# Steady groups: two visits of scores with seven PSUM banks each, one bank shared by both heads of a pair, in place of visits with six and eight

## The chip, the cores and the metric

The kernel runs on one core of a Trainium2 chip. Its time is the device time of one execution in microseconds (us), as a median over several runs. Before the change it is 344.38 us, the median of four runs from 344.21 to 344.92.

## What is computed

Sliding-window attention with ALiBi bias for 8 batches of 8 heads, 576 positions of 64 features each, and behind it a gated feed-forward block over the 4608 resulting rows of 512 features. Cut to what matters:

```python
scores = scale * q @ k.T                      # scale 1/8
mask = (rel >= 0) & (rel < 128)               # rel = query - key
attn = exp(scores + bias) under the mask, divided by its sum over the keys
x = attn @ v                                  # (4608, 512) over all heads
out = (gelu(x @ w_gate) * (x @ w_val)) @ w_out
```

## The kernel before

Engines: PE multiplies matrices into PSUM, ACT takes exponentials, gelu and copies, DVE does elementwise work, SP issues output transfers and transposing transfers. PSUM is one pool of eight banks of 128 x 512 fp32. Every result of PE takes a bank from it, `bank()`, and gives it back when its last reader is done; a new result waits for the reader whose bank it is given. The order on every engine is the order in which the code is written.

The feed-forward block runs over nine groups `g` of 512 rows. A group has twelve pairs of gate and value tiles (`gate_val`, L514: eight matmuls of 512 columns and two banks each; gelu on ACT, L520; the product with the value tile on DVE, L521) and four output tiles (`out_part`, L550: twelve matmuls of 512 columns into one bank; the copy out of PSUM by DVE or ACT, L555). The store of a finished output tile (L540, on SP) is issued at the start of the next call of `out_part`.

Attention for later batches is put between these output tiles, so that PE has work while ACT and DVE do theirs. A steady group (g = 2 to 5, batch b = g + 2) ends with the list that `steps(g)` gives: one output tile; the products of the batch before with its values (`values`, L392); a first visit of `scores` for pair 0; an output tile; a visit for pairs 1 to 3; an output tile; a visit for all four pairs; the sums of probabilities (`add`, on DVE); an output tile. The number 4 stands for one output tile (four calls' worth of three matmuls). In the next group, after three pairs of gate and value tiles, `sums4` (L334) takes the column sums.

Keys are taken in blocks of 128, n = 0 to 4, each with the 192 queries of its window (64 for the last block). `scores(b, s, cs)` covers blocks 0 and 1 for s = 0 and blocks 2, 3 and 4 for s = 1, for the pairs of heads in `cs`. For each pair it takes two banks, one for each head. Matmuls (L187, 64 keys by up to 192 queries) come in fours: head i of the pair takes the half i of PE's rows, and half x of the key block takes half x of PE's columns and of the bank's partitions. Then ACT takes the exponential of each bank (L192, 384 columns for s = 0, 448 for s = 1) into the probabilities `P`, and DVE multiplies both heads of the pair by the mask `emask` (L195). In banks, the three visits of a steady group take two, six and eight.

A PE matmul can be made to wait for another PE matmul through `relay`: a no-operation on another queue (SP in steady groups) waits for the first matmul, and the second one waits for it (`depends`). Before the change, only the products use this (L320), where one bank is written by both halves of PE's rows, one after the other.

Of the kernel before, what the change touches and what calls it, by code (L numbers as in the profile page):

```python
# [27 lines left out]
def kernel(  # L28
# [10 lines left out]
    nc = tc.nc  # L39
# [23 lines left out]
    def bank():  # L63
        return psum.tile([128, 512], FP32, name="ps")


    def keep_busy(ps, n, w=64):
        for _ in range(n):
# [17 lines left out]
    emask = consts.tile([128, H, 448], BF16, name="emask")  # L86
# [4 lines left out]
    qT, kT = ([consts.tile([128, 4, 640], BF16, name=f"{nm}T{i}") for i in range(2)]  # L91
              for nm in "qk")
# [81 lines left out]
    def prob(b):  # L174
        return Ps[b % 2].rearrange("p (c i) n -> p c i n", i=2)


    def keys(b, c, m):
        if b < 2:
            return kT[b][:, c, 64 * m:64 * m + 64]  # L180
        at = 512 * (m // 2) + 128 * c + 64 * (m % 2)
        return kT[b % 2].rearrange("p c x -> p (c x)")[:, at:at + 64]


    def score(b, c, i, m, q0, n, out, first=True):
        half = slice(64 * i, 64 * i + 64)
        nc.tensor.matmul(  # L187
            out=out, lhsT=keys(b, c, m)[half, :], rhs=qT[b % 2][half, c, q0:q0 + n],
            start=first, stop=True, skip_group_check=not first)

    def exp(dst, src):
        nc.scalar.activation(out=dst, in_=src, func=AF.Exp, scale=0.125)  # L192

    def mask(dst, m):
        nc.vector.tensor_tensor(out=dst, in0=dst, in1=m, op=ALU.mult)  # L195


    def scores(b, s, cs, later=None):
        pss = []
        for c in cs:  # L200
            ps = [bank(), bank()]
            pss.append(ps)
            for n in ((0, 1), (2, 3, 4))[s]:
                w, col = 64 if n == 4 else 192, 192 * (n - 2 * s)
                for x in (0, 1):
                    for i in (0, 1):
                        score(b, c, i, 2 * n + x, 128 * n + 64 * x, w,
                              ps[i][64 * x:64 * x + 64, col:col + w])
        w = (384, 448)[s]
        for c, ps in zip(cs, pss):  # L210
            dst = prob(b)[:, c, :, 64 + 384 * s:64 + 384 * s + w]
            for i in (0, 1):
                exp(dst[:, i, :], ps[i][:, 0:w])
            args = (dst, emask[:, 2 * c:2 * c + 2, 0:w])
            if later is None:
                mask(*args)
            else:
                later.append(args)

# [12 lines left out]
    def scores0(cs, pss, between=None):  # L234
        for c, ps in zip(cs, pss):
            for n in range(3):
                for x in (0, 1):
                    q0 = 128 * n + 64 * x
                    w = min(192, 384 - q0)
                    for i in (0, 1):  # L240
                        score(0, c, i, 2 * n + x, q0, w,
                              ps[i][64 * x:64 * x + 64, 192 * n:192 * n + w], False)
        for c, ps in zip(cs, pss):
            for i in (0, 1):
                exp(prob(0)[:, c, i, 0:512], ps[i])
                if i == 0 and between:
                    between()


    def scores0_rest(cs, later):  # L250
        pss = []
        for c in cs:
            ps = [bank(), bank()]
            pss.append(ps)
            for n, skip, w, col in ((4, 0, 64, 0), (2, 64, 128, 64), (3, 0, 192, 192)):
                for x in (0, 1):
                    for i in (0, 1):
                        score(0, c, i, 2 * n + x, 128 * n + 64 * x + skip, w,
                              ps[i][64 * x:64 * x + 64, col:col + w])
        for c, ps in zip(cs, pss):  # L260
            dst = prob(0)[:, c, :, 512:896]
            for i in (0, 1):
                exp(dst[:, i, :], ps[i][:, 0:384])
            later.append((dst.rearrange("p i (n x) -> p i n x", x=192),
                          emask[:, 2 * c:2 * c + 2, 0:192].unsqueeze(2).to_broadcast((128, 2, 2, 192))))
# [42 lines left out]
    def in_turn(mms):  # L308
        by_group = [[m for m in mms if m[0] == g] for g in range(4)]
        return [ms[n] for n in range(max(map(len, by_group))) for ms in by_group if n < len(ms)]  # L310

    def depends(use, on):
        tc.add_manual_dep(use.ins, on.ins.name, mybir.DependencyInfo(
            mybir.DependencyClass.Sync, mybir.DependencyReason.DATA), reason="one bank, two halves")

    def relay(mm, engine=nc.sync):
        by = engine.nop()  # L320
        depends(by, mm)
        return by

    def sums4(b, s):
        first, w = shape(b, s)
# [33 lines left out]
    def products(b, banks):  # L359
# [19 lines left out]
        for n, (_, x, u, c, m, q0, q1, col, to, lo, hi) in enumerate(todo):  # L379
            begun.setdefault(u, x)  # L380
            half = slice(64 * x, 64 * x + 64)
            for i in (0, 1):
                rows = slice(64 * i, 64 * i + 64)
                if isinstance(c, int):
                    h = 2 * c + i
                    out = pss[u][rows, to + q0 - lo:to + q1 - lo]
                    lhsT = vb[b % 2][half, m // 2, 64 * h:64 * h + 64]
                else:
                    out = pss[u][rows, to:to + (c.stop - c.start) * (hi - lo)].rearrange(
                        "p (c x) -> p c x", x=hi - lo)[:, :, q0 - lo:q1 - lo]  # L390
                    lhsT = ones64[half, :]
                mm = nc.tensor.matmul(  # L392
                    out=out, lhsT=lhsT, rhs=prob(b)[half, c, i, col:col + q1 - q0],
                    start=all(t[2] != u for t in todo[:n]), stop=True, skip_group_check=True)
                if begun[u] != x and u in by:
                    depends(mm, by.pop(u))
            if begun[u] == x and all(t[1:3] != (x, u) for t in todo[n + 1:]):
                by[u] = relay(mm, nc.vector if b in (1, 2) else nc.sync)
# [82 lines left out]
    def products_rest():  # L481
        w = S - lo0
        pss = products(0, [(n, slice(2 * n, 2 * n + 2), lo0, S, 0) for n in (0, 1)] + [
            (2 + c // 2, c, lo0, S, w * (c % 2)) for c in range(4)])
        for n in (0, 1):
            nc.scalar.copy(out=recip[0][:, 2 * n:2 * n + 2, lo0:S],
                           in_=pss[2 + n][:, 0:2 * w].rearrange("p (c x) -> p c x", c=2))
        return pss
# [49 lines left out]
    def store():  # L538
        for args in stores:
            nc.sync.dma_start(**args)  # L540
        stores.clear()
# [63 lines left out]
    for h in (0, 2, 4, 6):  # L605
        for w, src in ((0, q), (1, k)):
            (nc.scalar if w and h == 0 else nc.sync).dma_start(  # L607
                out=raw[w][h // 4].rearrange("p (h x) -> p h x", h=4)[:, h % 4:h % 4 + 2, :],
# [24 lines left out]
    for x in (0, 1):  # L633
        half, to = slice(64 * x, 64 * x + 64), slice(64 * x, 64 * x + 192)
# [130 lines left out]
    pss = products_rest()  # L765
# [10 lines left out]
    for n in range(2):  # L776
        nc.gpsimd.dma_start(
            out=wo[:, 6 * n:6 * n + 6, :],
# [5 lines left out]
    for t in (qs[0], ks[0]):  # L784
# [5 lines left out]
    todo = {  # L790
        0: [("table",), ("s", 1, 0, (0, 1)), ("o", 0, 0, 0), ("o", 0, 1, 0), ("s", 1, 0, (2, 3)), ("o", 0, 0, 1), ("s", 1, 1, (0, 1)), ("o", 0, 1, 1), ("s", 1, 1, (2, 3), masks), ("pv+", 1, 0), 4, ("pv+", 1, 1), ("transposes", 2), 4],
        1: [("table",), ("s", 2, 0, (0, 1)), 3, ("s", 2, 0, (2, 3)), 2, ("s", 2, 1, (0, 1)), 2, ("s", 2, 1, (2, 3), masks), ("pv+", 2, 0), 3, ("pv+", 2, 1), 1, ("s", 3, 0, (0, 1)), 2, ("s", 3, 0, (2, 3)), 3, ("add", 3, 0), ("s", 3, 1, range(4))],
    }

    def steps(g):
        b = g + 2
        if g in todo:
            return todo[g]
        if b > B:
            return [16] if g < NG - 1 else [12, ("last", g)]  # L800
        if b == B:
            return [4, ("pv", b - 1), 12]
        return [("table",), 4, ("pv", b - 1), ("s", b, 0, (0,)), 4, ("s", b, 0, (1, 2, 3)), 4,
                ("s", b, 1, range(4)), ("add", b, 0), ("add", b, 1), 4]


    def exp_table():
        nc.scalar.preload_act_table_set("natural_log_exp_and_others")

    RUN = {"s": scores, "add": add, "sum4": sums4, "gather": gather, "spread": spread_dma, "pv": values, "pv+": values_and_sums,  # L810
           "masks": flush, "table": exp_table, "transposes": transposes_dma, "last": out_last, "o": out_half}

    for g in range(NG):
# [33 lines left out]
        for item in steps(g):  # L847
            if isinstance(item, int):
                out_part(g, item)
            else:  # L850
                RUN[item[0]](*item[1:])
        store()
# [35 lines left out]
```

## Time and profile before

| what | us |
|---|---|
| median of four runs | 344.38 |
| the profiled execution, its time | 344.47 |
| its span, first to last instruction | 342.7 |
| PE busy | 334.9 |
| DVE busy | 190.1 |
| ACT busy | 174.3 |
| POOL busy | 108.5 |
| matmuls of scores, L187 (656), busy | 19.0 |
| exponentials, L192 (128), busy | 55.9 |
| masks, L195 (60), busy | 34.8 |

The span is what the profile's instructions cover; the time adds what lies around it. Busy time counts instructions of an engine without their overlap; matmuls are pipelined and the profile models their ends. PE's clock was granted in full throughout (1.000).

The last part of the third steady group (g = 4), as the timeline has it:

| start, us | what |
|---|---|
| 195.58 | products of the batch before, and the visit of pair 0 |
| 197.57 | second output tile |
| 200.27 | visit of pairs 1 to 3, 24 matmuls, six banks |
| 200.89 | third output tile |
| 203.58 | visit of all pairs, 48 matmuls, eight banks |
| 204.77 | fourth output tile |
| 207.36 | gate and value tiles of the next group |

### The profile page before, as it was taken

How to read it: one execution, taken by the hardware profiler on the slowest of the kernel's cores; microseconds unless marked ns; L12 is line 12 of the kernel's file. 1: busy time of each engine (PE TensorE's matmuls, PEld its weight loads, DVE VectorE, ACT ScalarE, POOL GpSimd, SP SyncE). 2: the span in 40 equal slices, each digit the busy share in tenths (PEclk: the TensorE clock that was granted, in tenths of full speed). 3: DMA queues.
4: the chain of work that ended last, by engine and by line, in shares of the span. 5: the costliest groups of instructions: out<-in, count | busy, mean ns of one | idle time of the engine just before them, and what ended most of it. 6: DMA issues, size and time to landing. Idle time of an engine off the chain costs nothing.

```text
span 342.7 us, 8079 instructions
## 1 busy us (share of the span) xinstructions
PE 334.9 (98%) x3310; PEld 170.7 (50%) x3310; DVE 190.1 (55%) x331; ACT 174.3 (51%) x339; POOL 108.5 (32%) x147
## 2 busy tenths in 40 slices
PE   8889999999999999999999999999999999999996
PEld 6567655444544455445544554445444544444443
DVE  8779565535599555944595369636773313303420
ACT  6884597537894339333753366344823133224322
POOL 9874763581193193009500770050000000000000
PEclk9999999999999999999999999999999999999999
DMA  8999999999599999989987999587114110020002
GB/s 210 169 197 190 205 163 137 149 191 174 124 161 128 190 168 195 175 178 86 182 175 157 94 178 185 138 100 97 63 36 104 63 65 0 0 94 31 0 31 94
DMA packets 149737, 43.48 MB, mean 127 GB/s; under 512 B 133540, under 2 KB 142660, under 8 KB 149700
## 3 DMA queue, kind: packets, MB, share of 16 engines
q0 software_dynamic: 107424, 18.10, 68.5%
q1 hardware_dynamic: 39104, 18.69, 22.9%
q10 hardware_dynamic: 3172, 6.19, 8.1%
q8 instruction: 26, 0.43, 0.5%
q14 instruction: 11, 0.09, 0.1%
HBM read 43.65 MB, written 9.53 MB: 155 GB/s over the span
## 4 chain that ended last, share of the span: by engine, by line
PE 90%; ACT 6%; DMA 2%; SPq 1%; issue 0%; DVE 0%; ACTq 0%
PE ps L514 54%; PE ps L550 25%; PE ps L392 4%; ACT P L192 3%; PE ps L187 2%; DMA ks<-in_k_dram 2%; PE ps L570 2%; PE ps L334 1%; ACT osb L555 1%; SPq L607 1%; PE ps L584 1%; PE ps L143 1%; ACT rb L468 0%; ACT rb L467 0%; ACT L520 0%
## 5 line engine op out<-in xcount | busy, mean ns | idle before, releaser
L521 DVE TENSOR_TENSOR hT<-ps,gelu 128x512 bf16<-128x512 f32 (+3 forms) x119 | 74.1, 636 | 92.1 <-PE ps L514 80.7
L520 ACT ACTIVATE gelu<-ps 128x512 bf16<-128x512 f32 (+3 forms) x119 | 65.4, 558 | 103.5 <-PE ps L514 90.4
L514 PE MATMUL ps<-xT,wg 128*128 128x512 bf16 (+3 forms) x476 | 113.5, 359 | 0.6 <-DVE xT L471 0.3
L514 PE MATMUL ps<-xT,wv 128*128 128x512 bf16 (+3 forms) x476 | 113.4, 359 | 0.0
L550 PE MATMUL ps<-wo,hT 128*128 128x512 bf16 x396 | 90.4, 379 | 0.2
L514 PEld LDWEIGHTS <-wv 128*128 128x128 bf16 x476 | 45.3, 98 | 48.5
L514 PEld LDWEIGHTS <-wg 128*128 128x128 bf16 x476 | 44.7, 98 | 48.6 <-issue 0.6
L192 ACT ACTIVATE P<-ps 128x384 bf16<-128x384 f32 (+2 forms) x128 | 55.9, 549 | 15.2 <-PE ps L187 15.0
L550 PEld LDWEIGHTS <-hT 128*128 128x128 bf16 x396 | 37.2, 98 | 44.2
L195 DVE TENSOR_TENSOR P<-P,emask 128x768 bf16<-128x768 bf16 (+1 forms) x60 | 34.8, 588 | 22.9 <-ACT P L192 22.0
L101 POOL DMA_DIRECT2D vb<-in_v_dram x40 | 33.9, 874 | 7.4 <-DMA ks<-in_k_dram 3.9
L555 ACT COPY osb<-ps 128x512 f32<-128x512 f32 x28 | 16.8, 599 | 36.6 <-PE ps L550 36.5
L101 POOL DMA_DIRECT2D qs<-in_q_dram x30 | 25.2, 855 | 6.2 <-DMA wo<-in_moe_w_out_dram 4.4
L839 POOL COPY mark<-hT 1x2 bf16<-1x2 bf16 x4 | 0.7, 176 | 79.2 <-DVE hT L521 79.2
L101 POOL DMA_DIRECT2D ks<-in_k_dram x30 | 25.6, 891 | 0.0
L187 PE MATMUL ps<-qT,kT 64*64 64x192 bf16 (+2 forms) x656 | 19.0, 236 | 0.2
L392 PE MATMUL ps<-P,vb 64*64 64x64 bf16 (+2 forms) x752 | 17.8, 221 | 0.3 <-SPq L320 0.2
L449 DVE TENSOR_TENSOR xT<-ps,rb 128x512 bf16<-128x512 f32 (+3 forms) x29 | 14.3, 563 | 6.6 <-PE ps L392 6.6
L187 PEld LDWEIGHTS <-kT 64*64 64x64 bf16 x656 | 13.1, 106 | 9.8 <-issue 7.8
L392 PEld LDWEIGHTS <-vb 64*64 64x64 bf16 x752 | 14.9, 107 | 4.2 <-issue 2.7
L276 DVE TENSOR_TENSOR T<-P 64x1024 bf16<-64x1024 bf16 (+1 forms) x20 | 15.0, 751 | 0.4
L425 DVE TENSOR_TENSOR xT<-ps,rb 128x512 bf16<-128x512 f32 (+1 forms) x10 | 6.4, 638 | 6.8 <-ACT rb L420 6.7
(86 smaller groups left out, 170.8 us busy)
## 6 DMA issues: line engine op xcount, KB each, us to landing
out_dram<-osb SPq DMA_DIRECT2D x35, 256.0 KB
rb<-rd ACTq DMA_DIRECT2D x10, 576.0 KB
vb<-in_v_dram POOLq DMA_DIRECT2D x32, 128.0 KB, 6.8
qs<-in_q_dram POOLq DMA_DIRECT2D x24, 128.0 KB, 5.0
ks<-in_k_dram POOLq DMA_DIRECT2D x24, 128.0 KB, 6.9
wo<-in_moe_w_out_dram POOLq DMA_DIRECT2D x2, 768.0 KB, 14.7
wg<-in_moe_w_gate_dram POOLq DMA_DIRECT2D x5, 256.0 KB, 8.5
wv<-in_moe_w_val_dram POOLq DMA_DIRECT2D x5, 256.0 KB, 9.4
```

The costliest lines, as they stand in the source:

```text
L101: nc.gpsimd.dma_start(out=t[0:n, j, :].rearrange("p (h d) -> p h d", h=H), in_=src[b][:, 128 * j:128 * j + n, :].rearrange("h p d -> p h d"))
L187: nc.tensor.matmul(out=out, lhsT=keys(b, c, m)[half, :], rhs=qT[b % 2][half, c, q0:q0 + n], start=first, stop=True, skip_group_check=not f ...
L192: nc.scalar.activation(out=dst, in_=src, func=AF.Exp, scale=0.125)
L195: nc.vector.tensor_tensor(out=dst, in0=dst, in1=m, op=ALU.mult)
L276: nc.vector.tensor_tensor(out=to[half, :, 2 * n0 + x:2 * n1 + x - 1:2], in0=P[half, :, 3 * n0:3 * n1 - 2:3], in1=P[half, :, 3 * n0 + 1:3 * ...
L392: mm = nc.tensor.matmul(out=out, lhsT=lhsT, rhs=prob(b)[half, c, i, col:col + q1 - q0], start=all(t[2] != u for t in todo[:n]), stop=True, ...
L449: nc.vector.tensor_tensor(out=xT[:, c, at:at + e - a], in0=src, in1=recip[b][:, c, a:e], op=ALU.mult)
L514: nc.tensor.matmul(out=ps, lhsT=w[:, c, 128 * f:128 * (f + 1)], rhs=xT[:, c, t0 + lo:t0 + hi], start=begins, stop=(c == 3), skip_group_che ...
L520: nc.scalar.activation(out=gl[:, 0:n], in_=pg, func=AF.Gelu)
L521: nc.vector.tensor_tensor(out=hid[g][:, f, lo:hi], in0=pv, in1=gl[:, 0:n], op=ALU.mult)
L550: nc.tensor.matmul(out=acc[g], lhsT=hid[g][:, f, 128 * t:128 * (t + 1)], rhs=wo[:, f, :], start=(f == 0), stop=(f == NF - 1))
L555: (nc.vector.tensor_copy if g < B - 2 and t in by_dve.get(g, (0,)) else nc.scalar.copy)(out=osb, in_=acc[g])
```

## The change

The last two visits of a steady group are made by a new function, `scores7`. Each takes seven banks: six for pairs 1 to 3, and one, `both`, in which both heads of pair 0 stand side by side. Visit s = 0 computes blocks 0 and 1 of pairs 1 to 3, as before, and block 2 of pair 0; visit s = 1 computes blocks 2 to 4 of pairs 1 to 3 and blocks 3 and 4 of pair 0. Head 0 writes its part of `both` first, then its share of pairs 1 to 3; head 1 takes the same pieces with pair 0 at the end. A relay on SP holds head 1's first matmul into `both` until head 0's last one is done. ACT takes the exponential of `both` last, as one instruction over both heads (2 x 192 columns, then 2 x 256). Pair 0's second mask covers 448 columns of each head and is made in visit s = 1, after the others.

The first visit of the group and all other groups are as before. `depends` and `relay` are moved up in the file without a change.

```diff
+    def scores7(b, s):
+        both, pss = bank(), [[bank(), bank()] for _ in range(3)]
+        todo = ([], [])
+        for i in (0, 1):
+            ns, w = (((2, 192),), 192) if s == 0 else (((3, 192), (4, 64)), 256)
+            for n, m in ns:
+                todo[i].append((0, n, m, both, w * i + 192 * (n - ns[0][0])))
+            mine = [(c, n, 64 if n == 4 else 192, pss[c - 1][i], 192 * (n - 2 * s))
+                    for c in (1, 2, 3) for n in ((0, 1), (2, 3, 4))[s]]
+            todo[i][:] = mine + todo[i] if i else todo[i] + mine
+        last = None
+        for n in range(len(todo[0])):
+            for x in (0, 1):
+                for i in (0, 1):
+                    c, m, w, ps, col = todo[i][n]
+                    half = slice(64 * i, 64 * i + 64)
+                    mm = nc.tensor.matmul(
+                        out=ps[64 * x:64 * x + 64, col:col + w], lhsT=keys(b, c, 2 * m + x)[half, :],
+                        rhs=qT[b % 2][half, c, 128 * m + 64 * x:128 * m + 64 * x + w],
+                        start=True, stop=True)
+                    if ps is both and i == 0:
+                        last = mm
+                    if ps is both and i and last is not None:
+                        depends(mm, by)
+                        last = None
+            if last is not None and todo[0][n][3] is both and (
+                    n + 1 == len(todo[0]) or todo[0][n + 1][3] is not both):
+                by = relay(last)
+        w = (384, 448)[s]
+        for c, ps in zip((1, 2, 3), pss):
+            dst = prob(b)[:, c, :, 64 + 384 * s:64 + 384 * s + w]
+            for i in (0, 1):
+                exp(dst[:, i, :], ps[i][:, 0:w])
+            mask(dst, emask[:, 2 * c:2 * c + 2, 0:w])
+        n, at = ((192, 448), (256, 640))[s]
+        exp(prob(b)[:, 0, :, at:at + n], both[:, 0:2 * n].rearrange("p (i x) -> p i x", i=2))
+        if s:
+            dst = prob(b)[:, 0, :, 448:896]
+            mask(dst, emask[:, 0:2, 0:448])
+
+
...
-        return [("table",), 4, ("pv", b - 1), ("s", b, 0, (0,)), 4, ("s", b, 0, (1, 2, 3)), 4,
-                ("s", b, 1, range(4)), ("add", b, 0), ("add", b, 1), 4]
+        return [("table",), 4, ("pv", b - 1), ("s", b, 0, (0,)), 4, ("s7", b, 0), 4, ("s7", b, 1),
+                ("add", b, 0), ("add", b, 1), 4]
...
-    RUN = {"s": scores, "add": add, "sum4": sums4, "gather": gather, "spread": spread_dma, "pv": values, "pv+": values_and_sums,
+    RUN = {"s": scores, "s7": scores7, "add": add, "sum4": sums4, "gather": gather, "spread": spread_dma, "pv": values, "pv+": values_and_sums,
```

More of the change, by code (lines that the diff above doesn't have):

```diff
@@ L182, in keys, with depends, relay @@
         return kT[b % 2].rearrange("p c x -> p (c x)")[:, at:at + 64]
+    def depends(use, on):
+        tc.add_manual_dep(use.ins, on.ins.name, mybir.DependencyInfo(
+            mybir.DependencyClass.Sync, mybir.DependencyReason.DATA), reason="one bank, two halves")
+    def relay(mm, engine=nc.sync):
+        by = engine.nop()
+        depends(by, mm)
+        return by
     def score(b, c, i, m, q0, n, out, first=True):
@@ L310, in in_turn @@
         return [ms[n] for n in range(max(map(len, by_group))) for ms in by_group if n < len(ms)]
[L315 to L322, printed above, removed]
     def sums4(b, s):
```

## Prediction, made before the changed kernel was run

> **What bounds the kernel now.** I read the page's busy table first, then the chain of waits, then the timeline of one steady group (the third, 195 to 209 us), then narrow windows of PE alone.
>
> ```profile
> PE 334.9 (98%) x3310; PEld 170.7 (50%) x3310; DVE 190.1 (55%) x331; ACT 174.3 (51%) x339; POOL 108.5 (32%) x147
> PE 90%; ACT 6%; DMA 2%; SPq 1%; issue 0%; DVE 0%; ACTq 0%
> ```
>
> PE is the bound: 334.9 of 342.7 us busy, 90% of the chain. Only what shortens PE's queue, or lets it wait less, can count. The chain leaves PE once in each of the four steady groups, at the same place; in the third:
>
> ```profile
> 200.34 0.62 PE ps L187 x24
> 200.96 2.71 PE ps L550 x12
> 203.67 0.02 issue
> 203.69 0.59 ACT osb L555
> 204.27 0.46 ACT P L192
> 204.73 0.04 issue
> 204.77 2.75 PE ps L550 x12
> ```
>
> The visit of eight banks (48 matmuls of L187) isn't in this chain; in its place stand the copy of the out tile before it, and the first exponential behind that copy. The timeline shows why:
>
> ```profile
> 203.58 1.13 PE L187 MATMUL ps<-qT,kT 64*64 64x192 bf16 x48
> 203.69 0.59 ACT L555 COPY osb<-ps 128x512 f32<-128x512 f32 x1 [0.42 <-PE ps L550]
> 204.17 3.60 ACT L192 ACTIVATE P<-ps 128x448 bf16<-128x448 f32 x8
> 204.77 2.75 PE L550 MATMUL ps<-wo,hT 128*128 128x512 bf16 x12
> ```
>
> The visit takes all eight banks. Its last one (pair 3, head 1) held the out tile that ACT copies until 203.69 + 0.59 = 204.28, and the next out tile then needs a bank back from the visit itself, the one that the first exponential frees (its end and PE's start are 0.04 apart in the chain). So PE waits twice inside 1.19 us (203.58 to 204.77). How much of that is waiting comes from the earlier visit of 24, which waits for nothing:
>
> ```profile
> 200.27 0.69 PE L187 MATMUL ps<-qT,kT 64*64 64x192 bf16 x24
> 200.89 2.76 PE L550 MATMUL ps<-wo,hT 128*128 128x512 bf16 x12
> ```
>
> Matmuls run in sets of four (two heads by two key halves), one quadrant of the array each. In narrow windows the first set of this visit lasts 0.28, and 0.69 for six sets makes (0.69 - 0.28) / 5 = 0.082 for each further wide set (192 columns). In the visit of 48 the first eight matmuls last 0.36 and the first twelve 0.39, so a narrow set (64 columns) takes 0.03. The out tile starts 0.62 after the visit's start, 0.07 before its recorded end. An undisturbed visit of 48, with eight wide and four narrow sets, would hold PE for 0.28 + 7 x 0.082 + 4 x 0.03 - 0.07 = 0.90. It holds it for 1.19: **0.29 us of waiting per group**, 4 x 0.29 = 1.16 us in all. The four groups agree to 0.01 (131.78 to 132.97, 167.68 to 168.87, 239.48 to 240.67). That is the ceiling of what the change can bring.
>
> **The change part by part**, in the times of the third group.
>
> *First of the two visits: six banks become seven, six sets become seven.* One wide set more: +0.08. It is no new work, only brought forward. The out tile behind it would start at 200.27 + 0.70 = 200.97. Its bank changes too: before, it took one that DVE had freed; now every bank but one belongs to the visit, and in the changed kernel's order it waits for ACT's copy of the previous out tile. That copy is 200.37 + 0.59 = 200.96, and with the 0.04 of the chain PE starts at 201.00, not 200.89: +0.11, of it 0.03 a new wait. Out tile and switch take 2.69 (200.89 to 203.58) again, so the second visit starts at 203.69.
>
> *Second visit: eight banks become seven.* Its banks come from exponentials of the first visit, the shared one of that visit (freed last) going to pair 3. ACT's six exponentials there took 2.41 from 200.85; a seventh at (2.41 - 0.52) / 5 = 0.38 ends at 203.64, before the visit starts. No bank waits for the copy any more. Seven wide and four narrow sets, if heads stayed in step, would hold PE for 0.28 + 6 x 0.082 + 4 x 0.03 - 0.07 = 0.82. They don't: head 0 does pair 0 first and head 1 does it last, so in six of eleven sets a wide matmul stands beside a narrow one. Lower end: quadrants run free, 0.82. Upper end: each set lasts as long as its widest, ten wide and one narrow, 0.28 + 9 x 0.082 + 0.03 - 0.07 = 0.98. I take 0.91, between them: quadrants are freed one by one, but the queue issues in order, so one key half trails the other by a narrow matmul or two (when I step the 44 matmuls through four quadrants in this order, it comes out there). The next out tile starts at 203.69 + 0.91 = 204.60. Its bank is that of the out tile before, copied from 203.80 to 204.39, free for PE at 204.43: 0.17 of cover.
>
> *So the out tile starts at 204.60, not 204.77*: 0.17 gained. An out tile not held up before its start is recorded 0.01 longer (2.76 against 2.75), which leaves **0.16 per group, 0.64 over four**.
>
> *Exponentials and masks.* 16 exponentials a group, as before. The second visit has six of 448 and one of 512 columns, not eight of 448. With (3.60 - 0.58) / 7 = 0.43 apart they start at 204.28 and the seventh ends near 207.45; before, the eighth ended at 207.77. The shared bank is freed last, but the first gate and value tiles, at 207.20, take the banks that are freed first (about 204.8 and 205.3); the shared one goes to the sums of L334, 5 us later. Cover 2 us. DVE has the same eight masks, pair 0's last; its additions start some 0.2 earlier, as PE does, so the sums at 212.63 find their input no later. Hidden, cost nothing; without that cover a late addition would hold PE for its own lateness.
>
> *Relays.* Two per group, eight in all: SP waits for head 0's last matmul in the shared bank and lets head 1's weight load go. Behind SP's relay stand the store of the next out tile and no transpose; ahead of it a store whose copy ended 3 us earlier. Who waits is PE, with everything behind it.
>
> ```profile
> PEld L392 <- SPq L320: 1.2, 3, 0.4
> PEld L392 <- DVEq L320: 0.8, 4, 0.2
> ```
>
> The trace has 55 such relays in the products; three on SP ended a wait of PE's weight loads, 0.4 at the longest. A quick one: the matmul ends at 196.63, the one behind the relay starts at 196.77, 0.14 later. In the first visit the matmul ends at 200.27 + 0.27 = 200.54, so the relay comes at 200.68; the weight load that needs it goes one set ahead of the seventh set, at 200.70. That is 0.02 of cover, and the 0.03 bank wait behind it would swallow as much again. In the second visit seven sets lie between: 0.1 of cover. I take 0 for both; the bounds are 0 and 0.4 per first visit.
>
> The Trainium skill (TensorE: Matmul & The Clock Gate, Part 3: Packing small matmuls) speaks against the mixed sets: it says that matmuls keep their order in start and also in end, so that a narrow one could not finish ahead of a wide one issued before it. This trace has narrow matmuls of 191 ns beside wide ones of 247 ns in one stream, with ends that the profile only models. By the rule the second visit would be the 0.98 of the upper end and the gain 0.09 per group, 344.02 in all.
>
> *Sum.* The profiled execution took 344.47, of it 342.7 span; nothing outside the span changes. 344.47 - 0.64 = 343.83; the median of the four runs is 344.38, 0.09 lower, and from it I forecast **343.74**. Noise first: four runs spread over 0.7 us, and 0.2% (0.69 us) is about what can be told from no change here. The forecast lies at that edge, at 0.19%.
>
> **Rivals.**
>
> *Nearly the whole wait goes.* Heads slip past each other freely (0.82), the copy comes in time: 203.66 + 0.82 = 204.48, 0.29 less per group, 344.38 - 1.16 = 343.2. For it: the products mix 64, 128 and 192 columns in one stream, and the trace puts no wait of theirs down to width. Against it: issue in order.
>
> *It only moves the wait.* Sets in lockstep (0.98) and 0.05 of relay wait in each visit: 0.17 - 0.07 - 0.10 = 0, so 344.4. For it: covers of 0.02 and 0.1 are thin. Against it: the three late relays all stand in products where two or more followed each other on SP; here one stands alone.
>
> *Slower: the relay of the first visit is late.* Place: the weight load before the seventh set. Price: each 0.1 of lateness past 200.70 costs 0.1 per group, less the 0.03 that the copy hides. Up to 0.19 late it eats the gain; beyond 0.36 the kernel is slower by 0.69. At the 0.4 of the longest wait on an SP relay: 0.16 - 0.40 + 0.03 = -0.21 per group, 344.38 + 0.84 = 345.2. Against it: SP is idle then, its last store issued at 196.84.
>
> **How the numbers follow.** Forecast 0.58, its own range 0.05 to 0.25 per group, 343.4 to 344.2; nearly half of it, 0.27, beyond 0.69 us because the mixed sets and the bank wait may each come out cheaper. Whole wait gone 0.22; moved 0.06; slower 0.14. Faster: 0.27 + 0.22 = 0.49. Within 0.2%: 0.31 + 0.06 = 0.37. Slower: 0.14. The range 343.1 to 344.6 takes in the first three cases and the mild end of the last.
>
> **What would show it.** Right: in each steady group the chain stays on PE from the second visit into the out tile, without the copy and the exponential; the visit's 44 matmuls start near 203.69 less what earlier groups gained and the out tile 0.91 later; the first visit's out tile waits 0.03 for the copy. Wrong: idle time of PE's weight loads put down to SP within the new visits, the second visit at 0.98 or above, or gates waiting for the last exponential.

## The result, and the profile after

The changed kernel takes **343.86 us**, the median of 50 runs (342.96 to 348.08); beside it the kernel before takes 344.89, the median of 72. The ratio is 0.9975, 95% interval 0.9964 to 0.9987: faster by 0.25%, where 0.19% was forecast.

First the page of the changed kernel: the busy table, and the chain's shares by engine.

```profile
PE 334.6 (98%) x3310; PEld 170.3 (50%) x3310; DVE 189.7 (55%) x331; ACT 174.4 (51%) x339; POOL 108.6 (32%) x147
PE 91%; ACT 5%; DMA 2%; SPq 1%; issue 0%; DVE 0%; ACTq 0%
```

The work is what it was (3310 matmuls, 331 and 339 instructions on DVE and ACT); the chain's share on ACT went from 6% to 5%, and that on PE from 90% to 91%. Then the chain of waits in the third steady group (start, duration, engine and line; L251 are the new visits' matmuls, L593 the output tiles, L557 gate and value tiles, L377 the sums).

```profile
200.39 0.70 PE ps L251 x28
201.09 2.72 PE ps L593 x12
203.81 0.83 PE ps L251 x36
204.64 2.70 PE ps L593 x12
207.33 5.18 PE ps L557 x24
212.51 0.61 PE ps L377 x32
```

Before, this stretch left PE for 1.05 us through the copy and the first exponential (0.59 and 0.46). Now it stays on PE from the first of the two visits to the sums of the next group. The timeline of the same stretch shows what each engine does (L598 is the copy out of PSUM, L204 the exponential, L583 the store's issue).

```profile
200.32 0.77 PE L251 MATMUL ps<-qT,kT 64*64 64x192 bf16 x28
200.43 0.59 ACT L598 COPY osb<-ps 128x512 f32<-128x512 f32 x1 [1.82 <-PE ps L593]
200.91 2.80 ACT L204 ACTIVATE P<-ps 128x384 bf16<-128x384 f32 x7
201.04 3.76 SPq L583 DMA_DIRECT2D out_dram<-osb  x2
201.06 2.75 PE L593 MATMUL ps<-wo,hT 128*128 128x512 bf16 x12
203.74 0.90 PE L251 MATMUL ps<-qT,kT 64*64 64x192 bf16 x44
203.85 0.59 ACT L598 COPY osb<-ps 128x512 f32<-128x512 f32 x1
204.34 3.22 ACT L204 ACTIVATE P<-ps 128x448 bf16<-128x448 f32 x7
204.57 2.27 PEld L593 LDWEIGHTS <-hT 128*128 128x128 bf16 x12
204.57 2.76 PE L593 MATMUL ps<-wo,hT 128*128 128x512 bf16 x12
207.17 0.59 PE L557 MATMUL ps<-xT,wg 128*128 128x512 bf16 x2
```

The visit of seven banks holds PE from 203.74 to 204.57. The next output tile starts with its bank already free (the copy ends at 203.85 + 0.59 = 204.44, 0.13 earlier), and only 0.23 behind the first exponential's start, where before it stood behind that exponential's end. From the starts of PE's instructions in the trace, in the first steady group (the four groups agree to 0.001 in both kernels):

| from, to (us) | before | forecast | after |
|---|---|---|---|
| first of the two visits, third output tile | 0.621 | 0.73 | 0.743 |
| third output tile, second visit | 2.695 | 2.69 | 2.680 |
| second visit, fourth output tile | 1.189 | 0.91 | **0.828** |
| fourth output tile, gate and value tiles | 2.586 | 2.60 | 2.601 |
| sum | 7.091 | 6.93 | **6.852** |

So a group gains 7.091 - 6.852 = 0.239, and four gain 0.96 us, or 0.28% of 344.38, inside the interval of the measurement. The two profiled executions differ by only 0.5 in their spans (342.7 and 342.2), because the changed kernel's execution began later: in the chain its first keys took longer to come. From before, then from after:

```profile
3.81 5.71 DMA ks<-in_k_dram
```

```profile
3.81 6.25 DMA ks<-in_k_dram
```

These 0.54 us lie ahead of any changed instruction. From the first gate matmul to the last, the traces have 328.562 - 15.498 = 313.06 before and 328.145 - 16.033 = 312.11 after: 0.95, the 0.96 again to 0.01.

### The profile page after: what moved, and what is told of

It is laid out like the page before. It is cut to its first block, busy times and chain, and to the rows that moved or that the text cites. A ratio compares the mean times of both kernels' runs of the same rounds, so it can differ in the third digit from the quotient of the medians.

```text
span 342.2 us, 8088 instructions
## 1 busy us (share of the span) xinstructions
PE 334.6 (98%) x3310; PEld 170.3 (50%) x3310; DVE 189.7 (55%) x331; ACT 174.4 (51%) x339; POOL 108.6 (32%) x147
## 4 chain that ended last, share of the span: by engine, by line
PE 91%; ACT 5%; DMA 2%; SPq 1%; issue 0%; DVE 0%; ACTq 0%
PE ps L557 54%; PE ps L593 25%; PE ps L435 4%; ACT P L204 2%; DMA ks<-in_k_dram 2%; PE ps L251 2%; PE ps L613 2%; PE ps L199 2%; PE ps L377 1%; SPq L650 1%; PE ps L627 1%; PE ps L143 1%; ACT rb L511 0%; ACT rb L510 0%; ACT L563 0%
## 5 line engine op out<-in xcount | busy, mean ns | idle before, releaser
L557 PE MATMUL ps<-xT,wg 128*128 128x512 bf16 (+3 forms) x476 | 113.5, 359 | 0.6 <-DVE xT L514 0.3
L557 PE MATMUL ps<-xT,wv 128*128 128x512 bf16 (+3 forms) x476 | 113.4, 359 | 0.0
L593 PE MATMUL ps<-wo,hT 128*128 128x512 bf16 x396 | 90.4, 379 | 0.0
L557 PEld LDWEIGHTS <-wv 128*128 128x128 bf16 x476 | 45.3, 98 | 48.6
L557 PEld LDWEIGHTS <-wg 128*128 128x128 bf16 x476 | 44.7, 98 | 48.7 <-issue 0.6
L204 ACT ACTIVATE P<-ps 128x384 bf16<-128x384 f32 (+2 forms) x128 | 55.9, 547 | 15.2 <-PE ps L199 15.0
L593 PEld LDWEIGHTS <-hT 128*128 128x128 bf16 x396 | 37.0, 98 | 44.1
L598 ACT COPY osb<-ps 128x512 f32<-128x512 f32 x28 | 16.7, 596 | 35.6 <-PE ps L593 34.8
L435 PE MATMUL ps<-P,vb 64*64 64x64 bf16 (+2 forms) x752 | 17.8, 220 | 0.3 <-SPq L192 0.2
L492 DVE TENSOR_TENSOR xT<-ps,rb 128x512 bf16<-128x512 f32 (+3 forms) x29 | 14.3, 564 | 6.6 <-PE ps L435 6.6
L435 PEld LDWEIGHTS <-vb 64*64 64x64 bf16 x752 | 14.8, 107 | 4.3 <-issue 2.7
L199 PE MATMUL ps<-qT,kT 64*64 64x192 bf16 (+2 forms) x368 | 11.8, 236 | 0.2
L199 PEld LDWEIGHTS <-kT 64*64 64x64 bf16 x368 | 7.6, 106 | 6.4 <-issue 4.8
```

The source lines that it names most:

```text
L199: nc.tensor.matmul(out=out, lhsT=keys(b, c, m)[half, :], rhs=qT[b % 2][half, c, q0:q0 + n], start=first, stop=True, skip_group_check=not f ...
L435: mm = nc.tensor.matmul(out=out, lhsT=lhsT, rhs=prob(b)[half, c, i, col:col + q1 - q0], start=all(t[2] != u for t in todo[:n]), stop=True, ...
L492: nc.vector.tensor_tensor(out=xT[:, c, at:at + e - a], in0=src, in1=recip[b][:, c, a:e], op=ALU.mult)
L557: nc.tensor.matmul(out=ps, lhsT=w[:, c, 128 * f:128 * (f + 1)], rhs=xT[:, c, t0 + lo:t0 + hi], start=begins, stop=(c == 3), skip_group_che ...
L593: nc.tensor.matmul(out=acc[g], lhsT=hid[g][:, f, 128 * t:128 * (t + 1)], rhs=wo[:, f, :], start=(f == 0), stop=(f == NF - 1))
L598: (nc.vector.tensor_copy if g < B - 2 and t in by_dve.get(g, (0,)) else nc.scalar.copy)(out=osb, in_=acc[g])
```

## The experiments

Each run below is judged by these same segments in its trace, since most differences are near or below what the times can tell; where a run was timed, its ratio to the kernel before stands beside it. In the steady groups the granted clock was 1.000 in every trace. Two theories were to be told apart: the gain is the eighth bank's wait, less the costs that the forecast named; or the gain comes from elsewhere (order of the sets, exponentials, the shared bank).

**Same move, eight banks first, then six, nothing shared.** The two visits use the old function: pairs 1 to 3 with pair 0's later blocks in the first, pairs 1 to 3 in the second.

```diff
-("s7", b, 0), 4, ("s7", b, 1),
+("s", b, 0, (1, 2, 3)), ("s", b, 1, (0,)), 4, ("s", b, 1, (1, 2, 3)),
```

> The same 16 banks per group, split 2, 8, 6: pair 0's later blocks (two banks of 448 columns) move into the first of the two visits; nothing is shared, no relay, all sets of equal width. Theory (a visit of eight banks makes PE wait, whatever is in it; the gain came from having no such visit): the waits come back in the first visit: its last bank waits for the copy of the second output tile, and the third output tile for the first exponential behind that copy, so that the third output tile starts about 1.14 us after the visit's start instead of 0.74, and the second visit, of six banks, waits for nothing (0.71). About 0.28 us per group over the changed kernel, +1.1 us, that is within 0.2 us of the kernel before. Rival (the gain came from the mixed order, the shared bank or the joint exponential): also slow, but with the first visit undisturbed at 0.81 us and no wait of PE for ACT in it. Rival 2 (only the last visit matters, because the copy and the exponentials pile up there): no waits, 0.2 to 0.3 us per group faster than before, like the changed kernel.

Measured: 344.82, ratio 1.0025 (0.9998 to 1.0053). Segments 1.136 and 0.714, sum 7.130, which is 0.04 above before and 0.28 above the changed kernel. Its timeline, first visit:

```profile
203.35 0.55 PEld L199 LDWEIGHTS <-kT 64*64 64x64 bf16 x26 [0.42 <-DVE xT L492]
203.46 0.59 ACT L598 COPY osb<-ps 128x512 f32<-128x512 f32 x1 [1.82 <-PE ps L593]
203.94 3.29 ACT L204 ACTIVATE P<-ps 128x384 bf16<-128x384 f32 x8
204.09 0.22 PEld L199 LDWEIGHTS <-kT 64*64 64x64 bf16 x10 [0.20 <-issue]
204.49 2.75 PE L593 MATMUL ps<-wo,hT 128*128 128x512 bf16 x11
```

The last ten weight loads begin only at 204.09, 0.05 after the copy's end (203.456 + 0.586 = 204.042), although the idle time before them is put down to "issue". The output tile starts at 204.485, 0.05 after the first exponential's end at 204.434. Both waits have moved, with the eighth bank, to the first visit. The second visit of six banks, with none, holds PE 0.714. Eight banks are thus the cause wherever they stand.

**Seven, then eight, nothing shared in the second.** Pair 0's blocks 3 and 4 take a bank for each head; both heads go in step.

```diff
+    def scores8(b):
+        pss = []
+        for c in range(4):
+            ps = [bank(), bank()]
...
-("s7", b, 1),
+("s8", b),
```

> The changed kernel's first visit (seven banks, one shared), then a visit with eight: pair 0's blocks 3 and 4 in two banks of 256 columns, heads in step, no relay there. One bank more than the changed kernel and nothing else. Theory (the eighth bank is what costs): the last bank waits for the copy of the third output tile and the fourth output tile for the first exponential; it starts about 4.48 us after the first visit's start instead of 4.25: +0.23 us per group, +0.9 us over the changed kernel, about the time of the kernel before. Rival (what helps is that work is brought forward into the first visit, so that the second is shorter): most of the gain stays, not over +0.1 us per group.

Measured: 345.25, ratio 1.002 (0.9998 to 1.0041). Segments 0.743 and 1.061, sum 7.084, that is before's less 0.007. The same 44 matmuls as in the changed kernel cost 1.061 - 0.828 = 0.233 more. The trace places it: in the set that opens the last bank, one matmul starts at 205.805 and the other three from 206.020 on, 0.05 after the copy's end at 205.968; in the sets before it all four start within 0.02 of each other. The second wait that was expected, of the output tile for the first exponential, isn't there: the tile starts 0.122 after the visit's last matmul does, as in the changed kernel, and the exponential, of 256 columns only, ends at 206.255, 0.083 ahead of it. So the expected 0.23 came about through one wait, not two. A first visit of seven banks alone gains next to nothing; the bank that the second visit gives up is what pays.

**Seven and seven, nothing shared.** Pair 0's heads are parted: head 0 has all three later blocks in the first visit, head 1 in the second. No relay is needed; three sets of each visit have matmuls of one head alone.

```diff
+        for n in (2, 3, 4):
+            w, col = 64 if n == 4 else 192, 192 * (n - 2)
+            for x in (0, 1):
+                score(b, 0, s, 2 * n + x, 128 * n + 64 * x, w, alone[64 * x:64 * x + 64, col:col + w])
```

> Seven and seven banks without sharing: the first visit takes head 0's three later blocks of pair 0 in a bank of its own, the second head 1's. No relay. Work is the same, but these matmuls have no partner of the other head beside them. Theory (seven banks remove the waits; sharing is there to keep both heads' halves of the array filled): no wait for ACT in either visit, third output tile 0.81 us after the first visit's start (0.74 in the changed kernel), fourth 0.90 after the second's start (0.83): +0.14 us per group, +0.55 us over the changed kernel, 0.4 us faster than before. Rival (the unpaired matmuls cost nothing, since PE overtakes): as fast as the changed kernel. Rival 2 (the waits stay): as slow as before or slower.

Measured: 344.64, ratio 1.001 (0.9988 to 1.0032), which can't tell it from before; in the trace the segments are 0.813 and 0.911, sum 7.017, 0.074 better than before and 0.165 worse than the changed kernel. No output tile waits for a bank (the third starts at 200.724, 0.12 after the copy's end at 200.603). The sets without a partner cost 0.07 in the first visit and 0.083 in the second; the first is more like 0.11, since the changed kernel's 0.743 has a wait for the copy in it and its seven sets alone would take 0.70 by the prediction's sum.

**The relay behind a store.** SP issues the pending store of an output tile ahead of the relay, so the relay has to wait for that tile's copy.

```diff
+                store()
                 by = relay(last)
```

> The changed kernel with each relay behind the store of the output tile before it on SP's queue: the store waits for ACT's copy and takes 0.33 us to issue. Theory (the relay is free only because it comes before it is needed; beyond that each 0.1 us late costs 0.1 us): the relay of the first visit comes at about 201.40 on the changed kernel's clock in the third group instead of 200.65, needed at 200.76, so that the third output tile starts 0.6 us later; that of the second visit 0.5 us late: +1.1 us per group, +4.5 us over the changed kernel, about 3.5 us slower than before. Rival (head 1's last set can wait while the output tile's matmuls go ahead, so that the relay hides): under +0.2 us per group.

Measured: 349.02, ratio 1.0135 (1.0108 to 1.0162). Segments 1.363 and 1.392, sum 8.049: 0.62 and 0.56 more than in the changed kernel, 1.20 per group. Its waits (engine and line, releaser, us in total, times, longest), and the first visit on the timeline:

```profile
PEld L251 <- SPq L192: 4.5, 8, 0.6
PE ps L251 <- SPq L192: 2.8, 8, 0.4
```

```profile
203.03 0.33 SPq L584 DMA_DIRECT2D out_dram<-osb  x1
203.47 0.11 PEld L251 LDWEIGHTS <-kT 64*64 64x64 bf16 x3 [0.61 <-SPq L192]
```

This is the forecast's slower rival made real: all eight relays are now late, by 0.6 at most. In the changed kernel, the same view has no wait of L251 on SP; its relays from the products are the three that stood there before:

```profile
PEld L251 <- issue: 3.0, 7, 0.4
PEld L435 <- SPq L192: 1.2, 3, 0.4
```

The idle time put down to "issue" here, 0.42 at the head of a visit, is that of the weight loader while PE still runs the tile before.

**Aligned sets.** In the second visit head 1 takes the blocks of a pair in the order 2, 4, 3, which leaves no set of mixed widths (six of eleven in the changed kernel).

```diff
-for n in ((0, 1), (2, 3, 4))[s]]
+for n in ((0, 1), ((2, 3, 4), (2, 4, 3))[i])[s]]
```

> The changed kernel with head 1's blocks in the order 2, 4, 3 in the second visit, so that in each of the eleven sets both heads have the same width. Theory (a narrow matmul beside a wide one costs nothing, because the other head's next matmul overtakes): the second visit stays within 0.01 us of the 0.83 us from its start to the fourth output tile. Rival (mixed sets still cost something that the 0.83 hides): shorter by 0.02 us or more.

Measured in a single execution: segments 0.743 and 0.828, to the last digit the changed kernel's. Its time of 346.30 isn't read, since the granted clock of that execution was 0.989 in the mean, with its dips ahead of the steady groups.

**Badly aligned sets.** In the second visit head 0 takes its narrow matmuls first and head 1 last: eight of eleven sets are mixed.

```diff
+            if s:
+                mine.sort(key=lambda t: t[2] * (-1 if i else 1))
```

> The changed kernel with head 0's narrow blocks first and head 1's last in the second visit: in eight of the eleven sets a narrow matmul stands beside a wide one, and head 0 has to run up to four sets ahead of head 1 for both halves to stay filled. Theory (PE lets a matmul overtake others whose part of the array is busy, far enough ahead): 0.83 us from the visit's start to the fourth output tile, as in the changed kernel. Rival (each set lasts as long as its widest): 0.28 + 10 x 0.082 - 0.07 = 1.03 us, +0.2 us per group. Between (issue in order, as in the prediction's stepping, or a short reach ahead): 0.9 to 0.99 us.

Measured in a single execution: 0.828 once more for the visit, and 344.43 us. Sets in lockstep would take 0.28 + 10 x 0.082 - 0.07 = 1.03, since each has a wide matmul. The trace has head 0 starting its sixth set at 204.058, when head 1 has started three (its fourth at 204.103, its fifth at 204.185). Mixed sets cost the visit nothing.

The group behind it isn't free, though: it takes 35.81 from its first gate matmul to the next group's, 35.66 in the changed kernel, 0.14 more in each group. That lies in the column sums of the next group, behind the four segments. From this run, then from the changed kernel:

```profile
204.59 3.22 ACT L204 ACTIVATE P<-ps 128x448 bf16<-128x448 f32 x7
212.42 0.42 DVE L337 COPY T<-P 64x1024 bf16<-64x1024 bf16 x1
212.53 0.83 PE L379 MATMUL ps<-T,ones 128*32 128x128 bf16 x32
```

```profile
204.34 3.22 ACT L204 ACTIVATE P<-ps 128x448 bf16<-128x448 f32 x7
212.18 0.42 DVE L335 COPY T<-P 64x1024 bf16<-64x1024 bf16 x1
212.44 0.68 PE L377 MATMUL ps<-T,ones 128*32 128x128 bf16 x32
```

The first exponential starts 0.76 after the visit's start, not 0.59. Its bank, pair 1's first, is filled at 0.57 by head 0's seventh set, but the semaphore signal that ACT waits for comes at 0.74, once head 1's matmul ahead of it in the code has ended too (0.71). Exponentials, masks and additions follow as much later. The last addition ends at 212.840, and the second half of the sums, which needs it, starts at 212.895. In the changed kernel the addition ends at 212.597 and that half starts at 212.678, with no time lost.

**Four, six and six banks.** With no visit over six banks there would be neither a shared bank nor a bank wait, if the first visit could take two pairs.

```diff
-("s", b, 0, (0,)), 4, ("s7", b, 0), 4, ("s7", b, 1),
+("s", b, 0, (0, 1)), 4, ("s", b, 0, (2, 3)), ("s", b, 1, (0,)), 4, ("s", b, 1, (1, 2, 3)),
```

> No visit over six banks and nothing shared: the first visit of the group takes pairs 0 and 1 (four banks), the second pairs 2 and 3 and pair 0's later blocks (six), the last pairs 1 to 3 (six). Theory (PE waits wherever a visit asks for more banks than are free by then; the first visit stands behind the products, whose five banks DVE still has to read): the last two visits run undisturbed (0.65 and 0.71 us to their output tiles), but pair 1 in the first visit waits until DVE's second step there ends (197.90 on the clock of the kernel before) and the second output tile until its fourth ends (198.56): it starts 1.04 us later than in the kernel before. Over the group -0.44 + 1.04 = +0.6 us, +2.4 us in all over the kernel before, +3.4 over the changed kernel. Rival (only the size of a visit counts): no wait in any of the three visits, 0.3 us per group faster than before.

Measured: 346.88, ratio 1.0045 (1.0022 to 1.0067). The later visits have 0.651 and 0.714, sum 6.658, the best of all; but the first visit is held by the batch before (L435 its products, L492 DVE's division, which frees their banks):

```profile
197.95 0.79 PE ps L435 x26
198.74 0.02 issue
198.76 1.43 DVE xT L492 x4
200.19 0.04 issue
200.24 0.38 PE ps L593
```

The output tile behind that visit starts 1.451 after the visit does, 0.408 in the changed kernel: 1.04 later, as expected, in this group. A steady group takes 36.36 to 36.50 from its first gate matmul to the next group's, 35.66 in the changed kernel and 35.90 before: 0.46 to 0.60 lost against before in each group, 2.0 in four. The total was expected at 2.4 from this group; in the other three the tile starts 1.32 after the visit. The difference is DVE's: there it divides each of the two banks that are waited for in one instruction of 512 columns (1.29 for both), in this group in pieces of 192 and 320 columns (1.42).

**The relay on ACT.** ACT's queue holds the copy of an output tile just ahead of the relay.

```diff
-                by = relay(last)
+                by = relay(last, nc.scalar)
```

> The changed kernel with its relays on ACT's queue instead of SP's, each behind the copy of an output tile. If an engine's no-operation goes only when the work before it on the engine is done: on the changed kernel's clock in the third group the first relay would come at 201.01 (needed at 200.76), the second at 204.43 (needed at 204.33): third output tile 0.2 to 0.3 us later, fourth 0.1 to 0.2 us: +0.3 to 0.5 us per group. If it goes as soon as the copy has been started: relays at about 200.65 and 204.13 as on SP, and nothing changes (0.74 and 0.83 us).

Measured in a single execution: 343.87 us, segments 0.744 and 0.828, the changed kernel's. In the first visit the copy runs from 199.804 to 200.390, and the relay's event on ACT's queue from 200.016 to 200.033, inside it: the relay doesn't wait for the copy to end. So the choice of queue matters through what waits ahead of the relay, as the store shows, and not through an operation that is under way.

What happens without the relay wasn't tried, since both halves of PE's rows would then write one bank with nothing to order them. Of the versions measured, none beats the changed kernel.

## Why the prediction was right

*The wait and its cause: right.* It put 0.29 per group on the visit of eight banks: the copy that holds the eighth bank, then the first exponential that gives the next output tile one. Moving the eighth bank moved both waits (7.130), and giving it back in the second visit alone brought the wait for the copy back (1.061). The chain lost exactly those two pieces in the steady groups. A fifth visit of 48 matmuls, in the group before them, still has both (0.59 and 0.45, from 98.28 on before and from 98.81 on after): the change doesn't touch it.

*The first visit, +0.11: right.* Measured +0.122. The moved set and the short new wait for the copy are both seen: the copy ends at 201.012 and the output tile starts at 201.062. The 0.05 between the two, not the 0.04 taken from the chain, is the rest.

*The second visit, 0.91: the mis-sized term.* It measured 0.828, the forecast's lower end of 0.82. The step that failed is "the queue issues in order": the middle was taken because one key half was to trail the other by a narrow matmul or two. The runs show no trailing. The order in the code (matmuls x0i0, x0i1, x1i0, x1i1; x the key half, i the head) isn't the order of starts. From the third set, where head 0's two are wide and head 1's narrow, the trace of the changed kernel has these starts (the head is told by the width, the key half by the order of starts; the trace names neither):

```
203.877  head 0, 192 columns, key half 0
203.884  head 0, 192 columns, key half 1
203.935  head 1, 64 columns, key half 0
203.941  head 1, 64 columns, key half 1
```

Head 0's quadrants came free after the narrow matmul of the set before, 0.028 after its start at 203.849; head 1's after a wide one, 0.083 after 203.852. The third matmul in the code went ahead of the second. Aligning the heads changed nothing in the visit and parting them further changed nothing in it, so 0.08 of the 0.24 gained in a group is this term: 0.91 - 0.828. The cover of the next output tile shrank with it: its bank is free for PE 0.05 after the copy's end, at 204.49, and the tile starts at 204.57, so 0.08 where 0.17 was forecast.

*Relays at no cost: right, and thin as it said.* In the first visit head 0's last matmul in the shared bank ends at 200.593, SP's event at 200.650, and the weight load that needs it starts at 200.761, in step with its neighbours: a cover of at most 0.11. In the second visit the event ends at 204.151 and the load starts at 204.330. The slower rival's price was about right where a store makes the relay late: in the first visit the load starts 0.71 later than in the changed kernel, and the output tile 0.62.

*Exponentials, masks and sums hidden: right, with next to no cover for the sums.* The gate and value tiles start 2.601 after the output tile, 0.015 more than before and with no wait on ACT or DVE in the chain; the sums follow from PE alone. The prediction gave 2 us of cover for the banks and no figure for the additions. The skewed run shows theirs: additions that end 0.157 later, counted from the visit's start, lengthen the sums by 0.141, so only some 0.02 was to spare.

*The sum.* 0.239 per group in place of 0.16 puts the result between the forecast and the rival "nearly the whole wait goes", nearer to that rival (0.29): the second visit went as the rival had it, the first as the forecast had it. That the median of 343.86 lies only 0.12 from the 343.74 of the forecast is partly luck: the gain was larger than forecast, and the kernel before came out at 344.89 over 72 runs, 0.51 above the median of four from which the forecast was reckoned.

## What to carry to other kernels

Where a stage takes every buffer of a pool, the user behind it waits for the first of that stage's own readers. One buffer fewer removes that wait, and it was worth 0.23 to 0.28 us a group here, also when matmuls had to be put out of step for it. A dependency passed through another engine's queue was free here where it came before it was needed (by 0.11 and 0.18 us) and nothing slow waited ahead of it: the same relay cost nothing on an idle SP or beside a running copy on ACT, and 0.6 us behind a store. When an order looks awkward for a tiled array, it pays to measure one that is worse, and to read the whole group: the skewed order cost its own visit nothing, and 0.14 us a group later, because the readers' first input came later.

## What the runs showed of the hardware

*Matmuls on different quadrants overtake each other in their starts, but not one that waits for a bank.* Two heads by two key halves of 64 x 64 ran as four streams. A visit of 44 matmuls took 0.828 in three orders, with none, six and eight of eleven sets mixed, where lockstep would have given up to 1.03. The Trainium skill (TensorE: Matmul & The Clock Gate, Part 3: Packing small matmuls) says that matmuls keep to program order in start and end. These starts don't: 203.884 lies ahead of 203.935, against the order of the code. The measurement decides, for this form of tiles. In the two cases below, the signals of finished matmuls do keep the order of the code. In the aligned run and in the changed kernel the matmul that fills pair 1's first bank starts 0.310 after the visit; it signals at 0.527 in the one and at 0.572 in the other, where a wide matmul of head 1 stands ahead of it in the code. In the skewed run such a matmul ends at 0.565 and signals at 0.738. Where a matmul waits for another engine, those behind it wait too: in the run with seven and eight banks the set that opens the last bank has one start at 205.805 and the other three at 206.020 to 206.027, though only head 1's two go into the bank that the copy held.

*A no-operation on ACT's queue passes while ACT is busy.* Its event at 200.016 lay within a copy from 199.804 to 200.390.

*From the end of an ACT read to PE's write of the bank it frees* it took 0.05 in each of these four cases (201.012 to 201.062, 204.042 to 204.092, 204.434 to 204.485, 205.968 to 206.020).
